# Another order of the opening's list, with 51 operations on other engines, in a chunked attention and two-layer expert kernel

## The chip, the core and the metric

The kernel runs on one core of a Trainium2 chip. A core has five engines that work side by side, each through its own instructions in the order in which they were written: PE (TensorE, matrix products and transposes), DVE (VectorE), ACT (ScalarE), POOL (GpSimd), and SP (SyncE), which here only issues DMAs. An instruction that must wait for another engine holds up everything behind it on its own engine. The metric is the time of one execution on the device in microseconds (us), median of several runs; less is better.

## The reference, cut to what matters

```python
# attention, per chunk of 32 queries: 8 memory keys, then 16 keys of left context, the chunk, 8 of right context
scores = scale * q_c @ k_full^T;  a = softmax(scores);  out[chunk] = a @ v_full      # (4, 8, 768, 64)
x = out as (3072, 512)
h = x @ w_in                                     # 512 -> 1024
solu = h * softmax(h);  ln = (solu - mean) / sqrt(var + 1e-6) * g_ln
x = ln @ w_out                                   # 1024 -> 512
h = x @ w2_in;  out = (h * clip(h + 3, 0, 6) / 6) @ w2_out    # 512 -> 2048 -> 512
```

The four weight matrices arrive as 64-bit floats, and the kernel turns them into 32-bit floats with integer operations. Products are made from a high part and a low part of each operand (three products for one).

## The kernel before, in words

The 3072 tokens are 24 tiles of 128. A tile passes through attention, the first layer and the second layer's first product; three tiles form a group for the product with `w_out`. The last stage, from about 423 us on, works through the 2048-wide layer and is not touched.

The work of the first seven tiles, the opening, stands in one list of names, `FIRST` (line 24 on). A loop near the end of the program calls one function for each entry, in the list's order; every function only appends instructions to its engines. So the list sets the order of the instructions on each engine and nothing else does: an engine never takes a later entry before an earlier one. From tile 7 (`STEADY`) a loop writes the instructions of each tile in a fixed pattern. A letter at an entry's end names its engine: A for ACT, D for DVE, P for POOL.

The entries that the text speaks of, with a tile number or a weight unit as the first argument:

- `load_q`, `load_k`, `load_v`, `load_mem_k`, `load_w1`, `load_wo`: DMAs, all issued by SP in the list's order. A `load_w1` is one of eight units of `w_in` (512 KB in two DMAs); unit u covers the columns u // 4 and the input rows u % 4. `load_k` is two DMAs (about 304 KB), `load_q` one of 256 KB, `load_v` eight to sixteen of 40 to 56 KB or less. There are two buffers for q, k and v, so `load_k:2` waits until `k_p:0` has read buffer 0.
- `w1_abs` (A or D), `w1_hold` (D or P), `w1_bits:u,0..2` (DVE): the conversion of one unit from 64 bits. `w1_hi` copies the rounded high part, `w1_lo` subtracts it (the low part). `wo_...` and `w2_...` do the same for the other weights, and `wo_g` multiplies by `g_ln`.
- `q_p`, `k_p`, `mem_p` (PE transposes of queries, keys, memory keys), with `q_e`, `k_e`, `mem_e`, `k_mem` as the copies out of the accumulator; `s_p` (PE, scores), `s_max`, `s_sub`, `s_sum` (DVE), `s_exp` (ACT), `s_norm` (D or P); `p_p` (PE transposes of the weights of attention, out of tile `pn`), `p_e` (copies), `v_p` (PE, attention output). `x_h` and `x_l` split that into high and low part.
- `m1:i,f,half` (PE): tile i times `w_in`, columns f, 12 matmuls or 6 for one half of the input rows. It needs `w1_hi` and `w1_lo` of its units and `x_h`, `x_l` of its tile. The first layer's nonlinearity and normalization follow as `ln_max` to `ln_norm`, `ln_p` (PE transposes), `ln_h`, `ln_l`; then `m2:g,piece` (PE, 8 matmuls with `w_out`).
- `warm:n` (PE, line 871): n transposes of the identity into a buffer that nobody reads. They compute nothing.
- `zero` clears buffers.

Of the kernel before, what the change touches and what calls it, by code (L numbers as in the profile page):

```python
# [22 lines left out]

STEADY = 7
FIRST = """
    load_q:0 load_w1:3 warm:10 q_p:0 warm:14 load_mem_k:0 mem_p:0 warm:6 mem_e:0,A zero:km0,D zero:v0,D zero:qb,P
    q_e:0,0,D w1_abs:3,D zero:kn0,P zero:kn1,D load_k:0 k_p:0,1 load_w1:7 load_mem_k:2 load_mem_k:3 load_w1:1 load_q:1
    w1_hold:3,P q_e:0,1,D k_p:0,0 warm:6 k_e:0,0,D k_mem:0,D mem_p:3 k_e:0,1,A s_p:0 warm:5 w1_abs:1,A w1_abs:7,A
    q_p:1 warm:8 q_e:1,1,A q_e:1,0,A zero:km1,D load_k:1 load_w1:0 load_k:2 load_w1:2 load_q:2 load_v:0 load_w1:6
    load_w1:5 load_w1:4 w1_bits:3,0 w1_bits:3,1 w1_hold:1,D mem_e:3,D w1_bits:3,2 s_edge:0 k_p:1,1 mem_p:2 k_p:1,0  # L30
    warm:6 s_max:0 w1_bits:1,0 s_sub:0 mem_e:2,A k_e:1,1,A k_e:1,0,A s_exp:0 s_p:1 warm:4 w1_abs:0,A w1_abs:2,A
    k_p:2,0 warm:6 k_e:2,0,A spread_mem_v:0,0,A zero:v1,P w1_hold:7,P w1_bits:7,0 w1_bits:1,1 w1_bits:7,1 w1_bits:1,2
    w1_bits:7,2 s_sum:0 w1_hold:0,D w1_bits:0,0 w1_bits:0,1 w1_hi:3,P s_norm:0,D zero:pb,P p_p:0 warm:6 q_p:2 load_k:3
    load_q:3 load_mem_k:1 load_q:4 load_v:1 p_e:0,0,A p_e:0,1,A spread_mem_v:0,64,A k_p:2,1 v_p:0 w1_bits:0,2
    w1_hi:1,D s_max:1 s_sub:1 s_exp:1 q_e:2,0,D x_h:0,0 k_e:2,1,D w1_hi:7,A w1_abs:6,A w1_abs:5,A w1_hold:2,P
    q_e:2,1,D s_p:2 warm:8 s_sum:1 w1_bits:2,0 w1_bits:2,1 s_norm:1,D p_p:1 warm:4 w1_bits:2,2 p_e:1,0,A w1_abs:4,A
    p_e:1,1,A w1_hi:2,A w1_lo:1,P w1_lo:3,P s_max:2 w1_hold:5,D x_l:0,0 w1_hold:4,D w1_bits:5,0 w1_bits:4,0
    w1_bits:5,1 load_k:4 load_wo:4 load_g load_v:2 consts w1_hi:0,P w1_lo:0,P w1_hold:6,P w1_lo:7,P w1_lo:2,P
    load_wo:2 m1:0,0,0 early_open k_p:3,1 k_p:3,0 k_e:3,1,A q_p:3 k_e:3,0,A q_e:3,1,A q_e:3,0,A w1_bits:4,1 s_sub:2
    w1_bits:6,0 w1_bits:5,2 mem_p:1 m1:0,0,1 s_p:3 q_p:4 w1_bits:6,1 w1_bits:4,2 w1_hi:4,D w1_bits:6,2 w1_lo:4,D  # L40
    w1_hi:5,P spread_mem_v:1,0,A s_exp:2 spread_mem_v:1,64,A v_p:1 w1_hi:6,D s_sum:2 s_max:3 s_norm:2,D s_sub:3
    q_e:4,1,A x_h:1,0 q_e:4,0,A mem_e:1,A w1_lo:5,P m1:0,1,0 w1_lo:6,P k_p:4,1 m1:0,1,1 x_l:1,0 k_e:4,1,D p_p:2
    k_p:4,0 m1:1,0,0 s_exp:3 ln_max:0 wo_abs:4,A wo_hold:4,D s_sum:3 wo_bits:4,0 s_norm:3,P load_wo:0 load_k:5
    load_wo:1 p_e:2,0,A k_e:4,0,A s_p:4 m1:1,0,1 ln_exp:0 p_e:2,1,A v_p:2 wo_abs:2,A wo_bits:4,1 ln_den:0 s_max:4
    ln_solu:0 wo_abs:0,D x_h:2,0 wo_hold:0,D wo_bits:4,2 s_sub:4 x_l:2,0 ln_mean:0 p_p:3 m1:1,1,0 k_p:5,0 m1:1,1,1
    m1:2,0,0 k_p:5,1 m1:2,0,1 s_exp:4 k_e:5,0,A ln_sq:0 p_e:3,0,A p_e:3,1,A wo_bits:0,0 s_sum:4 wo_g:4 wo_hold:2,P
    wo_bits:0,1 wo_hi:4,D ln_var:0 k_e:5,1,A wo_abs:1,A ln_max:1 wo_bits:0,2 ln_exp:1 wo_bits:2,0 ln_pow:0 wo_hold:1,D
    wo_bits:2,1 s_norm:4,P ln_norm:0 ln_den:1 load_q:5 load_v:3 load_k:6 m1:2,1,0 q_p:5 v_p:3 q_e:5,1,A q_e:5,0,A
    x_h:3,1 p_p:4 p_e:4,0,A load_wo:5 load_q:6 wo_abs:5,A p_e:4,1,A s_p:5 ln_p:0,0 ln_h:0,0,1 k_p:6,1 m1:2,1,1 k_p:6,0
    wo_bits:2,2 wo_g:0 ln_solu:1 ln_mean:1 wo_bits:1,0 wo_bits:1,1 wo_hi:0,D k_e:6,1,A q_p:6 k_mem:6,D ln_sq:1  # L50
    load_v:4 load_wo:7 v_p:4 load_q:7 load_wo:3 load_k:7 ln_max:2 wo_g:2 s_edge:5 q_e:6,1,A ln_exp:2 ln_var:1
    k_e:6,0,D wo_hi:2,D s_max:5 wo_lo:4,P x_l:3,1 wo_lo:0,P m1:3,0,0 x_h:4,1 ln_p:0,1 m1:3,0,1 m1:3,1,0 wo_hold:5,P
    q_e:6,0,A ln_den:2 wo_lo:2,D wo_bits:1,2 s_sub:5 s_p:6 q_p:7 k_p:7,0 m1:3,1,1 ln_l:0,0,1 x_l:4,1 ln_pow:1
    ln_solu:2 wo_bits:5,0 m1:4,0,0 wo_abs:7,A s_exp:5 ln_h:0,1,1 wo_hold:7,D wo_g:1 s_sum:5 s_norm:5,P s_edge:6
    wo_bits:5,1 ln_mean:2 k_e:7,0,A wo_abs:3,A wo_hold:3,P ln_l:0,1,1 ln_sq:2 wo_hi:1,A q_e:7,0,A q_e:7,1,A ln_norm:1
    ln_p:1,0 m1:4,0,1 k_p:7,1 p_p:5 m1:4,1,0 ln_max:3 ln_exp:3 ln_h:1,0,1 ln_p:1,1 m1:4,1,1 k_e:7,1,A wo_bits:5,2
    wo_lo:1,P load_v:5 load_wo:6 p_e:5,0,A wo_abs:6,D s_max:6 ln_den:3 ln_var:2 ln_pow:2 ln_l:1,0,1 s_sub:6 s_exp:6
    p_e:5,1,A ln_h:1,1,1 ln_l:1,1,1 ln_norm:2 wo_bits:3,0 ln_solu:3 load_k:8 k_p:8,1 ln_p:2,0 ln_h:2,0,1 ln_l:2,0,1
    s_p:7 k_e:8,1,A load_v:6 load_q:8 v_p:5 early_close k_p:8,0 ln_p:2,1 m2:0,0 wo_bits:3,1 wo_hold:6,D ln_max:4
    ln_exp:4 x_h:5,1 k_e:8,0,A s_sum:6 s_norm:6,P x_l:5,1 p_p:6 q_p:8 wo_bits:6,0 ln_den:4 ln_mean:3 ln_solu:4 m1:5,0  # L60
    s_max:7 wo_g:5 wo_bits:3,2 wo_g:3 wo_hi:5,P wo_lo:5,P wo_bits:6,1 wo_hi:3,D m1:5,1 s_sub:7 ln_mean:4 ln_h:2,1,1
    ln_l:2,1,1 q_e:8,1,A ln_sq:3 wo_lo:3,D wo_bits:6,2 m2:0,1 wo_bits:7,0 ln_var:3 wo_g:6 wo_bits:7,1 wo_bits:7,2
    wo_g:7 load_k:9 p_e:6,0,A p_e:6,1,A v_p:6 q_e:8,0,A ln_pow:3 ln_norm:3 wo_hi:6,A wo_lo:6,P s_exp:7 s_p:8 wo_hi:7,A
    wo_lo:7,P m2:0,2 m2:0,3 ln_p:3,0 m2:0,4 ln_p:3,1 x_h:6,1 ln_max:5 s_sum:7 x_l:6,1 s_norm:7,D p_p:7 m2:0,5 ln_sq:4
    ln_exp:5 ln_h:3,0,1 ln_h:3,1,0 ln_den:5 ln_solu:5 m1:6,0 ln_l:3,0,1 s_max:8 m2_e:0,0 m2:0,6 m2:0,7 m1:6,1 load_v:8
    load_w2:1 w2_abs:1,A w2_hold:1,P w2_bits:1,0 ln_mean:5 p_e:7,1,A ln_sq:5 p_e:7,0,D ln_var:5 ln_var:4 w2_bits:1,1
    ln_pow:4 ln_pow:5 w2_bits:1,2 ln_l:3,1,0 ln_norm:4 ln_p:4,1 load_v:7 v_p:7 ln_max:6 m2_e:0,1 s_sub:8 ln_norm:5
    ln_p:4,0 m2:0,8 m2:0,9 ln_exp:6 ln_h:4,1,0 x_h:7,0 ln_den:6 ln_l:4,1,0 ln_p:5,1 m2:0,10 ln_solu:6 x_l:7,0
    ln_mean:6 ln_p:5,0 m2:0,11 load_w2:3 w2_store:1 w2_abs:3,A s_exp:8 s_sum:8 ln_sq:6 ln_var:6 w2_hold:3,P ln_pow:6
    s_norm:8,P ln_norm:6 ln_h:5,1,0 load_w2:0 m2_s:0,1 w2_abs:0,A ln_h:4,0,0 w2_hold:0,P ln_l:4,0,0 ln_l:5,1,0  # L70
# [1016 lines left out]
```

## Time and profile before

| what | value |
|---|---|
| median of 3 runs (lowest, highest) | 924.26 us (923.72, 926.64) |
| the profiled execution | 925.95 us, its span 923.9 us |
| PE busy, share of the span | 903.0 us, 98% |
| DVE, ACT, POOL busy | 594.2, 450.5, 431.2 us |
| opening: start to the first matmul of tile 7 | 0 to 133.45 us |
| first matmul with `w_in` (tile `h`) | 33.92 us |

The span runs from the first to the last instruction that the profiler saw; 2.05 us of the execution lie outside it. "Busy" on PE includes the identity transposes. A row of the timeline gives start, length, engine, line, operation, tiles and, in square brackets, the time that the engine stood idle before it, with what ended that. PEclk is the clock granted to TensorE as a share of its full 2.4 GHz.

### The profile page before, as it was taken

Reading aid. Unit: us, or ns where it says so; the run is one execution under the profiler, and the core shown is the slowest. Engines: PE = TensorE matmul, PEld = TensorE weight load, DVE = VectorE, ACT = ScalarE, POOL = GpSimd, SP = SyncE. Lnnn points to the kernel's source line nnn. Section 1 sums busy time; section 2 is a strip of 40 time slices with the busy share of each in tenths; the row PEclk is TensorE's granted clock in tenths of the full one; section 3 lists DMA queues with packets and bytes.
Section 4 is the critical chain, followed back from the end, with each engine's and each line's share of the span. In section 5 each row is a group of like instructions: output and inputs, shape, how many; then the busy total and the mean of one; then the engine's idle time right before and its main releaser. Section 6 shows DMA issues by size and latency. Waiting matters only on the chain.

```text
span 923.9 us, 20340 instructions
## 1 busy us (share of the span) xinstructions
PE 903.0 (98%) x7823; PEld 848.0 (92%) x7823; DVE 594.2 (64%) x1043; ACT 450.5 (49%) x802; POOL 431.2 (47%) x465
## 2 busy tenths in 40 slices
...
GB/s 201 186 226 131 56 112 177 224 189 244 216 210 225 195 252 174 145 263 272 223 209 156 200 87 206 134 173 164 181 181 106 206 113 174 185 169 175 122 183 103
DMA packets 175627, 165.13 MB, mean 179 GB/s; under 512 B 107436, under 2 KB 128428, under 8 KB 175148
## 3 DMA queue, kind: packets, MB, share of 16 engines
...
q14 instruction: 33, 0.27, 0.1%
...
## 4 chain that ended last, share of the span: by engine, by line
PE 75%; DVE 10%; DMA 4%; issue 4%; POOL 3%; SPq 1%; ACT 1%; DVEq 0%; POOLq 0%; ACTq 0%
PE ph L771 25%; PE acc L825 23%; PE m L616 11%; PE h L531 9%; PE tp L588 2%; PE sc L444 2%; PE tp L500 1%; DMA b2d<-b_km 1%; PE tp L482 1%; DMA pair<-w2d 1%; PE tp L431 1%; SPq L193 1%; DMA w2raw<-in_moe_w_out_dram 1%; DVE so L557 1%; DVE so L581 1%
## 5 line engine op out<-in xcount | busy, mean ns | idle before, releaser
L531 PE MATMUL h<-w,xh 128*128 128x512 f32 x336 | 108.5, 403 | 1.0 <-DVE w L307 0.6
L616 PE MATMUL m<-lnh,wol 128*128 128x384 f32 x256 | 88.1, 344 | 1.0 <-POOL wol L344 0.7
L616 PE MATMUL m<-lnh,woh 128*128 128x384 f32 x256 | 87.9, 343 | 0.5 <-ACT woh L218 0.5
L616 PE MATMUL m<-lnl,woh 128*128 128x384 f32 x256 | 87.9, 343 | 0.0
L786 POOL TENSOR_TENSOR b_pe<-b_pe 128x128 f32<-128x128 f32 x48 | 27.0, 562 | 129.9 <-DVE b_pe L783 129.9
L786 POOL TENSOR_TENSOR b_pn<-b_pn 128x128 f32<-128x128 f32 x48 | 26.5, 552 | 124.0 <-DVE b_pn L783 123.1
L531 PEld LDWEIGHTS h<-w,xh 128*128 128x128 f32 x336 | 60.0, 188 | 12.7 <-DVE w L307 0.9
L246 DVE TENSOR_TENSOR b_ll<-b_xh,b_lh 128x512 fp32r<-128x512 f32 x48 | 33.2, 692 | 58.1 <-ACT b_lh L245 58.1
L576 POOL TENSOR_TENSOR lst<-lst,constants 128x1 f32<-128x1 f32 x24 | 15.2, 634 | 117.9 <-DVE lst L571 114.7
L771 PE MATMUL ph<-b_xah,b_wa 128*128 128x256 f32 x384 | 69.4, 276 | 0.0
L771 PE MATMUL ph<-b_x2r,b_wa 128*128 128x256 f32 x384 | 69.3, 276 | 0.0
L231 POOL TENSOR_SCALAR w2t<-w2t 128x512 f32<-128x512 f32 x32 | 62.1, 1947 | 14.3 <-ACT w2t L224 13.8
L246 DVE TENSOR_TENSOR b_wb<-b_xh,b_wb 128x512 fp32r<-128x512 f32 x48 | 38.5, 802 | 45.5 <-ACT b_wb L245 45.5
L531 PE MATMUL h<-w,xl 128*128 128x512 f32 x168 | 66.2, 394 | 1.3 <-DVE xl L261 1.3
L245 ACT ACTIVATE b_wb<-b_xh 128x512 fp32r<-128x512 f32 x48 | 30.3, 632 | 60.3 <-POOL b_xh L788 60.3
L771 PEld LDWEIGHTS ph<-b_xah,b_wa 128*128 128x128 f32 x384 | 59.6, 188 | 0.0
L771 PEld LDWEIGHTS ph<-b_x2r,b_wa 128*128 128x128 f32 x384 | 59.6, 188 | 0.0
L246 DVE TENSOR_TENSOR b_ll<-b_pe,b_lh 128x384 fp32r<-128x384 f32 x48 | 28.1, 586 | 47.6 <-ACT b_lh L245 47.5
L245 ACT ACTIVATE b_lh<-b_xh 128x512 fp32r<-128x512 f32 x48 | 30.3, 632 | 58.0 <-POOL b_xh L788 58.0
L246 DVE TENSOR_TENSOR b_xal<-b_pn,b_xah 128x384 fp32r<-128x384 f32 x48 | 26.8, 559 | 48.4 <-ACT b_xah L245 48.4
L245 ACT ACTIVATE b_xah<-b_pn 128x384 fp32r<-128x384 f32 x48 | 25.2, 525 | 60.8 <-POOL b_pn L786 59.5
L771 PE MATMUL ph<-b_xal,b_wa 128*128 128x256 f32 x192 | 53.0, 276 | 0.0
...
## 6 DMA issues: line engine op xcount, KB each, us to landing
...
```

The lines of the kernel that those rows point to most:

```text
L193: SP.dma_start(out=dst[r0 + NM + lo - s0:r0 + NM + hi - s0, j], in_=v[b, h0:h0 + 4, lo:hi, :].rearrange("h t d -> t h d"),)
L231: ENG[eng].tensor_scalar(out=tf, in0=tf, scalar1=U_LO, scalar2=U_HI, op0=ALU.max, op1=ALU.min)
L245: ACT.activation(out=hi, in_=r, func=AF.Copy)
L246: (eng or DVE).tensor_tensor(lo, r, hi.bitcast(F32), ALU.subtract)
L444: PE.matmul(sc[64 * x:64 * x + 64, c, s], qb[:, p, c].rearrange("k y t -> k (y t)"), kT[i % 2][:, p, c], start=True, stop=True)
L531: PE.matmul(h[:, f], a[:, kt], w[kt][:, f * 512:(f + 1) * 512], start=n == 0, stop=n == 3 * NKT - 1)
L576: POOL.tensor_tensor(st[:, 10:11], st[:, 9:10], mhalf, ALU.pow)
L588: PE.transpose(pt[:, c], so[:, fc * P:(fc + 1) * P], ident)
L616: PE.matmul(acc, w[fc // 2][:, fc % 2, dc * P:(dc + 1) * P], a[:, fc], start=n == 0, stop=n == len(todo) - 1)
L771: PE.matmul(ph[:, k], w[:, wl, dc * P:(dc + 1) * P], xg[gi][xl][dc], start=m == 0, stop=m == len(todo) - 1)
L786: POOL.tensor_tensor(q[:, 6], q[:, 0], q[:, 3], ALU.add)
L825: PE.matmul(out, a[al][:, blk], w[:, wl], start=j == 0 and m == 0 and PLACE[p][1] == 0, stop=j == NS - 1 and m == 2, skip_group_check=True)
```

## The change

`FIRST` is replaced as a whole; nothing else in the program differs. Both lists hold the same operations on the same data, except for the identity transposes: 83 in twelve entries before, 118 in ten entries now. 51 entries name another engine: from DVE to ACT 14, from DVE to POOL 15, from ACT to DVE 6, from POOL to DVE 7, from POOL to ACT 4, from ACT to POOL 5. DVE is thus rid of 29 and given 13, POOL is rid of 11 and given 20, ACT is rid of 11 and given 18. The order differs nearly everywhere; of the table the diff shows little:

```diff
-    load_q:0 load_w1:3 warm:10 q_p:0 warm:14 load_mem_k:0 mem_p:0 warm:6 mem_e:0,A zero:km0,D zero:v0,D zero:qb,P
+    zero:kn1,D zero:km1,D load_q:0 zero:v0,D zero:qb,P load_w1:0 load_mem_k:0 zero:kn0,P zero:km0,D load_k:0
...
+    warm:30 s_p:1 load_w1:7 w1_bits:6,1 w1_abs:4,A w1_hi:5,A load_k:2 w1_hi:0,A warm:3 q_p:2 s_norm:0,P s_max:1
+    w1_hold:4,D warm:27 k_p:2,0 load_q:3 w1_bits:4,0 w1_abs:7,A k_p:2,1 w1_bits:4,1 zero:pb,P s_sub:1 q_e:2,0,A
...
```

SP's list now begins with: `load_q:0`, `load_w1:0`, `load_mem_k:0`, `load_k:0`, `load_k:1`, `load_w1:5`, `load_q:1`, `load_w1:6`, `load_w1:4`, `load_q:2`, `load_w1:7`, `load_k:2`, `load_q:3`, `load_w1:2`, `load_k:3`, `load_v:0`, `load_w1:1`, `load_k:4`, `load_q:4`, `load_mem_k:3`, `load_w1:3`, `load_v:1`, `load_wo:1`, `load_k:5`. Before, the units of `w_in` came as 3, 7, 1, 0, 2, 6, 5, 4, and the second, third and fourth key tile behind more of them.

Place one is PE around the scores of the second tile (`s_p:1`). `idle` is the tile of the identity transposes, `sc` that of the scores, `q_raw`, `kn0` and `km` hold queries and keys as loaded. Before:

```order
L871 MATMUL idle_359<-ident_73 128x128 x6
L444 MATMUL sc_375<-kT_142,qb_140 64x64 x16
L871 MATMUL idle_392<-ident_73 128x128 x4
L402 MATMUL tp_399<-ident_73,kn0_135 128x128
L403 MATMUL tp_399<-ident_73,km_137 128x24
```

Now:

```order
L431 MATMUL tp_301<-ident_73,q_raw_246 128x128 x4
L871 MATMUL idle_318<-ident_73 128x128 x30
L444 MATMUL sc_349<-kT_142,qb_140 64x64 x16
L871 MATMUL idle_377<-ident_73 128x128 x3
L431 MATMUL tp_381<-ident_73,q_raw_316 128x128 x4
L871 MATMUL idle_391<-ident_73 128x128 x27
```

60 identity transposes stand where 10 stood, and `q_p:2` is drawn ahead of the third tile's keys.

Place two is PE ahead of the first matmul with `w_in` (tile `h`); `pn` is read by `p_p:1`, `v0` by `v_p:0`. Before:

```order
L500 MATMUL tp_473<-pb_141,v0_138 64x2x32 x16
L444 MATMUL sc_507<-kT_142,qb_140 64x64 x16
L871 MATMUL idle_524<-ident_73 128x128 x8
L482 MATMUL tp_540<-ident_73,pn_538 128x128 x4
L871 MATMUL idle_545<-ident_73 128x128 x4
L531 MATMUL h_592<-w1_240,xh_498 128x512 x2
```

Now the keys of the fifth tile (`k_p:4`, eight instructions, of which the first two stand here) lie between `p_p:1` and `h`:

```order
L871 MATMUL idle_545<-ident_73 128x128 x5
L500 MATMUL tp_551<-pb_141,v0_138 64x2x32 x16
L444 MATMUL sc_576<-kT_142,qb_140 64x64 x16
L482 MATMUL tp_593<-ident_73,pn_500 128x128 x4
L871 MATMUL idle_598<-ident_73 128x128 x2
L402 MATMUL tp_601<-ident_73,kn0_135 128x128
L403 MATMUL tp_601<-ident_73,km_137 128x24
```

`sc_507` holds the scores of the third tile, `sc_576` those of the fourth: one more tile has been transposed and scored before `h` begins.

Place three is DVE around `x_l:0` (line 261, tile `xl`), which the first `h` matmuls need. `w1raw` holds units of `w_in` in conversion: line 226 is `w1_abs`, 231 `w1_hold`, 235, 238 and 241 are `w1_bits`. Before:

```order
L456 TENSOR_REDUCE ast_557<-sc_507 128x8
L231 TENSOR_SCALAR w1raw_239<-w1raw_239 128x512
L261 TENSOR_TENSOR xl_499<-tp_473,xh_498 128x512
L231 TENSOR_SCALAR w1raw_312<-w1raw_312 128x512
L235 TENSOR_SCALAR w1raw_239<-w1raw_239 128x512
```

Now:

```order
L238 SCALAR_TENSOR_TENSOR w1raw_291<-w1raw_291 128x512
L226 TENSOR_SCALAR w1raw_242<-w1raw_242 128x512
L231 TENSOR_SCALAR w1raw_242<-w1raw_242 128x512
L261 TENSOR_TENSOR xl_607<-tp_551,xh_606 128x512
L235 TENSOR_SCALAR w1raw_242<-w1raw_242 128x512
L238 SCALAR_TENSOR_TENSOR w1raw_242<-w1raw_242 128x512
```

`xl` now stands behind the first two steps of unit 1 (`w1raw_242`), and so behind that unit's DMA.

## Rows read from the trace of the kernel before

**Rows 1.** The page, part 1: busy us (share of the span) and instructions of each engine

```profile
PE 903.0 (98%) x7823; PEld 848.0 (92%) x7823; DVE 594.2 (64%) x1043; ACT 450.5 (49%) x802; POOL 431.2 (47%) x465
```

**Rows 2.** Windows: stretch, its length, busy us of engines (instructions), PEclk, DMA share, GB/s

```profile
0.00:14.10 14.10, 11.99 (x96) 10.20 (x97) 5.90 (x11) 2.69 (x5) 4.86 (x10) 1.00 0.87 196
14.10:33.92 19.82, 14.90 (x174) 12.61 (x173) 18.43 (x34) 11.01 (x20) 12.76 (x12) 0.91 0.94 213
33.92:112.00 78.08, 73.48 (x681) 56.59 (x680) 76.75 (x136) 54.60 (x97) 44.39 (x33) 1.00 0.58 141
112.00:133.45 21.45, 21.45 (x152) 20.00 (x152) 14.64 (x34) 10.81 (x20) 7.79 (x8) 1.00 0.45 128
133.45:423.00 289.55, 288.47 (x2405) 257.07 (x2405) 230.40 (x422) 160.62 (x295) 115.74 (x95) 1.00 0.71 209
```

**Rows 3.** Waits of PE, 0 to 133.4 us: us in total, times, longest

```profile
PE tp L482 <- DVE pn L474: 4.1, 2, 3.0
...
PE h L531 <- DVE xl L261: 1.3, 1, 1.3
...
PE h L531 <- DVE w L307: 0.6, 1, 0.6
```

**Rows 4.** Timeline of PE, 0 to 134 us: start, length, line, operation, count, idle before

```profile
1.34 2.40 PE L871 MATMUL idle<-ident 128*128 128x128 f32 x10 [1.34 <-POOL ident masks.py:199]
...
17.54 0.87 PE L871 MATMUL idle<-ident 128*128 128x128 f32 x6
...
24.62 1.12 PE L482 MATMUL tp<-ident,pn 128*128 128x128 f32 x4 [3.04 <-DVE pn L474]
...
33.92 0.71 PE L531 MATMUL h<-w,xh 128*128 128x512 f32 x2
...
36.95 0.27 PE L402 MATMUL tp<-ident,kn 128*128 128x128 f32 x1
...
38.60 0.66 PE L431 MATMUL tp<-ident,q_raw 128*128 128x128 f32 x4
39.19 0.41 PE L389 MATMUL tp<-ident,mk 8*128 8x8 f32 x4
39.52 0.73 PE L531 MATMUL h<-w,xh 128*128 128x512 f32 x2
...
41.11 1.15 PE L444 MATMUL sc<-kT,qb 128*64 128x64 f32 x32
...
133.45 0.63 PE L531 MATMUL h<-w,xh 128*128 128x512 f32 x2
```

**Rows 5.** Groups by line and shape, DVE, 0 to 150 us: busy us, mean ns, idle before

```profile
L235 DVE TENSOR_SCALAR w1raw<-w1raw 128x512 uint32<-128x512 uint32 x8 | 5.8, 735 | 0.1
...
L474 DVE TENSOR_TENSOR pn<-pe,ast 128x512 f32<-128x512 f32 x4 | 3.2, 789 | 0.0
L220 DVE COPY qb<-tp 64x512 f32<-64x512 f32 x4 | 2.8, 688 | 3.6 <-PE tp L431 3.5
...
L220 DVE COPY kT<-tp 128x448 f32<-128x448 f32 x4 | 2.5, 620 | 1.4 <-PE tp L403 1.4
L220 DVE CAST woh<-woraw 128x512 fp32r<-128x512 f32 x3 | 2.4, 784 | 0.0
```

**Rows 6.** The same view for POOL

```profile
L231 POOL TENSOR_SCALAR w1raw<-w1raw 128x512 f32<-128x512 f32 x4 | 8.6, 2155 | 14.3 <-ACT w1raw L224 9.3 <-DVE w1raw L226 5.0
...
L474 POOL TENSOR_TENSOR pn<-pe,ast 128x512 f32<-128x512 f32 x5 | 5.6, 1114 | 10.9 <-DMA kn<-in_k_dram 6.0 <-DVE ast L470 4.9
```

**Rows 7.** Timeline of DVE, 11 to 18 us

```profile
11.46 0.35 DVE L235 TENSOR_SCALAR w1raw<-w1raw 128x512 uint32<-128x512 uint32 x1
...
17.06 1.70 DVE L235 TENSOR_SCALAR w1raw<-w1raw 128x512 uint32<-128x512 uint32 x1
```

**Rows 8.** Timeline of POOL beside it

```profile
16.98 0.60 POOL L220 CAST w<-w1raw 128x512 fp32r<-128x512 f32 x1
17.53 0.95 POOL L856 MEMSET pb<- 128x1024 f32 x1
```

More of the change, by code (lines that the diff above doesn't have):

```diff
@@ L25 @@
 FIRST = """
-    load_q:0 load_w1:3 warm:10 q_p:0 warm:14 load_mem_k:0 mem_p:0 warm:6 mem_e:0,A zero:km0,D zero:v0,D zero:qb,P
[L27 to L70, printed above, removed]
@@ L71 @@
-    ln_h:5,0,0 ln_l:5,0,0 load_q:9 m2_s:0,0 m2_e:0,2 m2_e:0,3 m2_s:0,2 m2_s:0,3 load_v:9 load_k:10
+    zero:kn1,D zero:km1,D load_q:0 zero:v0,D zero:qb,P load_w1:0 load_mem_k:0 zero:kn0,P zero:km0,D load_k:0
+    w1_abs:0,D load_k:1 warm:26 mem_p:0 q_p:0 mem_e:0,A q_e:0,0,D warm:2 k_p:0,0 k_e:0,0,D k_mem:0,D q_e:0,1,A
+    w1_hold:0,P k_p:0,1 k_e:0,1,A load_w1:5 load_q:1 warm:6 s_p:0 w1_bits:0,0 k_p:1,1 w1_bits:0,1 w1_bits:0,2
+    w1_abs:5,D s_edge:0 k_p:1,0 k_e:1,0,A w1_hold:5,P s_max:0 load_w1:6 k_e:1,1,D s_sub:0 w1_bits:5,0 w1_abs:6,A
@@ new lines @@
+    load_w1:4 q_p:1 w1_bits:5,1 s_exp:0 q_e:1,1,D w1_bits:5,2 s_sum:0 w1_hold:6,P w1_bits:6,0 q_e:1,0,A load_q:2
+    warm:30 s_p:1 load_w1:7 w1_bits:6,1 w1_abs:4,A w1_hi:5,A load_k:2 w1_hi:0,A warm:3 q_p:2 s_norm:0,P s_max:1
+    w1_hold:4,D warm:27 k_p:2,0 load_q:3 w1_bits:4,0 w1_abs:7,A k_p:2,1 w1_bits:4,1 zero:pb,P s_sub:1 q_e:2,0,A
+    s_exp:1 w1_bits:6,2 w1_bits:4,2 load_w1:2 q_e:2,1,A s_sum:1 k_e:2,0,A w1_hold:7,P load_k:3 p_p:0 q_p:3 k_e:2,1,A
+    p_e:0,0,A w1_bits:7,0 load_v:0 w1_hi:6,P s_p:2 w1_bits:7,1 w1_hi:4,A w1_bits:7,2 w1_abs:2,A q_e:3,0,A w1_hold:2,D
```

37 lines of the change are left out of this document (added).

## The prediction

> **What bounds the kernel now.** I first looked at the busy shares of the page: PE is busy in 98% of the span [rows 1]. So the kernel is shortened only where PE waits, or where it works for nothing. The windows show where that is [rows 2]. The lengths of the first four windows less their busy time give 11.6 us without PE work up to 133.45 us, where tile 7 and the fixed loop begin [rows 4]. In the 289.55 us behind that PE lacks only 1.1 us, so whatever the opening gains arrives at the end nearly whole. Of the 11.6 us, 7.0 lie before the first `h` matmul at 33.92 us and 4.6 behind it. The first 1.34 us, until the identity exists, cannot go [rows 4]; 5.7 us are left of the early part, and 10.3 us in all.
>
> Who ends these waits? The view of PE's waits names DVE for the largest: 4.1 us for `pn` (the two `p_p`, 3.04 us of it ahead of the first), 1.3 us for `xl`, 0.6 us for a low part of `w` [rows 3]. That fits the windows: DVE is busy 18.4 of 19.8 us before the first `h` and 76.8 of 78.1 us behind it [rows 2]. From 112 us on DVE has time (14.6 of 21.5 us) and PE has no gap. The opening is thus bound by DVE's queue and PE together.
>
> **The change part by part.**
>
> *Identity transposes.* Six take 0.87 us, 0.145 us each [rows 4]; 35 more cost 35 x 0.145 = 5.1 us of PE time in any case, since they are instructions in line and are not skipped when the data is there. All other PE work is the same. So the most that the opening can gain is 10.3 - 5.1 = 5.2 us, and every wait that the new order has (beyond the 1.34 us) is taken off that: gain = 5.2 - early waits - late waits.
>
> *PE ahead of the first `h`.* The order puts two more key tiles, one query tile and one set of scores there, and two `mem_p` less. By the starts of neighbouring rows a key tile takes 38.60 - 36.95 = 1.65 us, a query tile 0.59, a `mem_p` 0.33, and the scores about 1.1 [rows 4]: 3.3 + 0.6 + 1.1 - 0.7 = 4.3 us. That is work drawn forward, not added. Without any early wait the first `h` would start at 33.92 - 5.7 + 5.1 + 4.3 = 37.6 us, against 33.92 + 4.3 = 38.2 for the same amount of work done before. The early part is therefore nearly a wash: 5.7 us of waits are exchanged for 5.1 us of identity transposes.
>
> *The waits that go.* `s_norm:0` and `s_norm:1` leave DVE's full queue for POOL, and `p_p:0` stands behind 60 identity transposes (8.7 us) and two more transposing steps, so its 3.04 us wait is covered. `x_l:0` now waits on DVE for unit 1 of `w_in`, and its reader is due at 37.6 us. SP has issued about 6.4 MB up to that unit (7 units of 0.52 MB, four query and four key tiles, one value tile). At the rates of the first two windows, 196 GB/s to 14.1 us (2.76 MB) and 213 GB/s after it [rows 2], it lands at 14.1 + 3.63 / 0.213 = 31.1 us; three DVE instructions of some 0.4 to 0.8 us later [rows 5] `xl` is there, at about 33. That wait (1.3 us) and that for the low part (0.6 us) should go too. What queues behind DVE's wait for unit 1 is that unit's own conversion and `s_sum:2`; their readers on PE come after the first twelve `h` matmuls.
>
> *The new early waits.* Two places can wait. `mem_p:0` is reached at about 6.7 us, and its data was used at 7.4 us before, with the same DMAs ahead: 0 to 0.7, I take 0.5. `k_p:5` stands behind `load_v:1` and a whole unit of `w_out` in SP's queue, 8.8 MB in all. PE reaches it about 8.3 us after the first `h` (three times six matmuls of 1.6 us, 0.6 + 0.3 + 1.1 + 1.1 + 0.4 for the rest), at 45.9. At 213 GB/s throughout it lands at 42.5 us; with 213 to 33.92 us and the 141 GB/s of the third window behind that [rows 2] at 46.9. So 0 to 1.0 us, I take 0.5. Early waits: 1.0 us.
>
> *DVE's load and the late waits.* DVE is rid of 16 instructions net, of 0.62 to 0.79 us by their groups [rows 5]: 16 x 0.7 = 11 us. POOL gets 9 net, at 1.1 us (`s_norm`) to 2.2 us (`w1_hold`) each [rows 6]: 10 to 19 us on top of the 70 us that it is busy in the opening [rows 2], so it has room. What POOL's instructions do to DVE is the cost that the diff hides. A `w1_bits` step that is 0.4 us short as a rule took 1.70 us from 17.06 us on [rows 7], and ended just behind two POOL instructions that ran from 16.98 to 18.48 us [rows 8]. Its group has a mean of 0.735 us [rows 5], so on average an instruction of that kind loses a quarter of what this one lost. If each of the 9 cost DVE nothing, DVE keeps 11 us; if each cost 1.3 us, 9 x 1.3 = 11.7 us eat all of it. I take a quarter, 3 us, nearest to the group's mean: DVE is about 8 us lighter, while PE comes to the same work at most 3 us earlier. Of the 4.6 us of late waits, 1.9 have gone above; of the other 2.7 I keep half, 1.3 us.
>
> The Trainium skill speaks against this change here: its page "SBUF — State Buffer", section "Who interferes with whom", says that VectorE in its two-port modes and GpSimd share one pair of ports as an exclusive lock, and that whichever is second stands still until the first has finished. Rows 7 and 8 agree with it for one instruction (1.70 us). Taken for all 9 it would return the whole 11 us to DVE; with the group's mean it returns 3 us. The rival on POOL below is what it would do here.
>
> *The end of the opening.* `load_v:8` is now issued last, behind the store of the last `w_out` result. Its reader stands some 10 us of PE work into the loop; I take it as covered.
>
> *Sum.* 5.2 - 1.0 - 1.3 = 2.9 us. The profiled execution would go from 925.95 us (span 923.9 us) to 923.05 us. It lies 1.7 us over the median of the three runs shown, which all lie within 3 us, so I take the difference off the median: 924.26 - 2.9 = 921.4 us. A measurement of this kernel can tell about 0.3%, 2.8 us, from no change, so this is just at that line.
>
> **The rivals.**
>
> *POOL takes back what DVE gives.* The 9 added POOL instructions block DVE fully, as the one at 17.06 us was. DVE's load is then 0.6 us above before, the late waits stay near 4.3 us, and the gain is 5.2 - 1.0 - 4.3 = -0.1: 924.4 us. For it: DVE is 97% full in the stretch where most of these instructions lie [rows 2]. Against it: the group's mean, and POOL is idle in more than a third of that stretch, so the instructions can fall beside DVE work that is not touched. The same time comes out if the change only swaps the owners of waits.
>
> *The loads come too late; slower.* In front of `h` PE now has identity transposes in place of waits that would shorten by themselves when something else is late. `k_p:5` and the value tile ahead of it hang on 8.8 MB, in a queue in which `load_v:1` must also wait for a clearing by POOL, behind four `w1_hold`. It decides below 6.05 / (45.9 - 14.1) = 190 GB/s after 14.1 us; at 150 GB/s, near the third window's 141, the keys land at 54.4 us, PE waits 8.5 us, and the gain is 5.2 - 0.5 - 1.3 - 8.5 = -5.1: 929.4 us. It passes the 0.3% line at about 159 GB/s. For it: the rate did fall to 141 GB/s from 33.92 us on. Against it: SP then asked for less (DMA share 0.58), and with more asked it gave 213 GB/s at 0.94.
>
> **How the numbers follow.** The forecast with its waits of 0.2 to 4.6 us, 919.1 to 923.7 us, gets 0.61, of which 0.45 lie below 921.5 (faster by over 0.3%) and 0.16 above. POOL's rival gets 0.25 (0.22 same, 0.01 faster, 0.02 slower), the late loads 0.14 (0.12 slower, 0.02 same). Faster 0.46, same 0.40, slower 0.14. The range runs from 918.6, just past the gain of 5.2 us, to 928.0, which leaves out the larger part of the late loads, about 1 in 10.
>
> **What would show it right or wrong.** In the profile of the changed kernel the first `h` matmul should start between 37.6 and 39.5 us and the first matmul of tile 7 at about 130.5 us. No wait of over 1 us should stand ahead of a `p_p` or for `xl`. DVE should be busy about 8 us less up to there. Waits of PE on the loads of keys or values of tiles 1 to 5 of several us mean the second rival. DVE's `w1_bits` and `wo_bits` with means above 0.9 us, and waits of PE on DVE, mean the first. The sum is wrong at its root if PE's gaps behind 133 us grow by what the opening saved.

## The result and the profile after

| | before | after |
|---|---|---|
| median of 6 runs (lowest, highest) | 924.62 us (923.72, 926.64) | 931.01 us (927.9, 931.8) |
| the profiled execution, its span | 925.95, 923.9 us | 931.8, 930.0 us |
| first matmul with `w_in` (`h`) | 33.92 us | 39.83 us |
| first matmul of tile 7, end of the opening | 133.45 us | 137.41 us |
| first matmul of the last stage (`ph`) | 423.79 us | 428.11 us |

The changed kernel is slower by 0.6%: ratio 1.006, 95% interval 1.0045 to 1.0075. Of the 6.1 us by which the span grew, 4.0 arise in the opening, and only 0.4 between it and the last stage. The other 1.7 us arise in the last stage, which the change does not touch; they are treated at the end.

Windows of the kernel after, with the columns and four of the five stretches of [rows 2] (stretch, length, busy us of PE, PEld, DVE, ACT, POOL with instructions, PEclk, DMA share, GB/s):

```profile
0.00:14.10 14.10, 11.39 (x96) 9.61 (x97) 8.02 (x16) 3.12 (x5) 5.56 (x10) 1.00 0.90 212
14.10:33.92 19.82, 17.42 (x207) 15.09 (x205) 19.30 (x27) 12.63 (x23) 15.37 (x13) 1.00 0.91 201
33.92:112.00 78.08, 72.33 (x648) 57.30 (x650) 66.08 (x116) 52.08 (x93) 49.31 (x40) 0.93 0.57 141
112.00:133.45 21.45, 20.81 (x164) 19.07 (x159) 15.99 (x31) 11.65 (x20) 10.04 (x9) 1.00 0.26 70
```

Length less PE's busy time gives 2.7 + 2.4 + 5.8 + 0.6 = 11.5 us without PE work, where it was 11.6 [rows 2]. So no wait was saved: they changed their owners and their places. By this count the opening is longer because PE is *busy* longer, 125.9 us up to 137.41 where it was 121.8 up to 133.45: 35 more identity transposes, and a granted clock of 0.93 in the third stretch (1.00 in [rows 2]; the 0.91 of the second stretch there is now 1.00). That says where the time stands and not yet what caused it; `e7_fewer` below shows that identity transposes can fill time that PE would otherwise have waited. DVE is busy 10.7 us less in the third stretch, where it now waits itself, and 0.9 us more in the second, where it was already full.

Waits of PE in the kernel after, 0 to 137.4 us (in total, times, longest), to be read against [rows 3]:

```profile
PE tp L402 <- DMA kn<-in_k_dram: 4.0, 1, 4.0
PE sc L444 <- DVE pe L461: 3.1, 2, 2.8
PE tp L389 <- DMA mk<-in_mem_k_dram: 1.4, 1, 1.4
...
PE m L616 <- POOL wol L344: 0.6, 1, 0.6
```

The waits for `pn`, `xl` and the low part of `w` are gone, as forecast. Two others stand in their place. The timeline of PE (start, length, line, operation, count, idle before) shows them, and what PE does behind them:

```profile
13.98 3.44 PE L871 MATMUL idle<-ident 128*128 128x128 f32 x30
17.35 1.15 PE L444 MATMUL sc<-kT,qb 128*64 128x64 f32 x32
...
34.86 1.88 PE L444 MATMUL sc<-kT,qb 128*64 128x64 f32 x32 [2.82 <-DVE pe L461]
...
51.88 0.30 PE L402 MATMUL tp<-ident,kn 128*128 128x128 f32 x1 [4.05 <-DMA kn<-in_k_dram]
...
53.01 1.22 PE L531 MATMUL h<-w,xh 128*128 128x512 f32 x2
...
58.43 1.36 PE L500 MATMUL tp<-pb,v 128*64 128x64 f32 x32
```

The same scores take 1.15 us at 17.35 and 1.88 behind the 2.82 us wait; the first two `h` matmuls behind the 4.05 us wait take 1.22 us instead of 0.73 [rows 4]. Both waits are followed by some microseconds at the lower of the two clock levels (1.2 instead of 2.4 GHz): the granted clock is 0.54 from 34.86 to 36.70 us and 0.50 from 53.01 to 58.43 us.

*Where the 4.05 us come from.* They stand ahead of `k_p:5`. SP's timeline in the kernel after (L320 is `load_wo`, L171 `load_k`), SP's own waits, and two windows with the columns as above:

```profile
37.28 2.54 SPq L193 DMA_DIRECT2D v<-in_v_dram  x4
46.56 0.36 SPq L320 DMA_DIRECT2D woraw<-in_moe_w_out_dram  x1
47.01 0.39 SPq L171 DMA_DIRECT2D kn<-in_k_dram  x1
```

```profile
SPq L320 <- POOL w L307: 3.7, 1, 3.7
SPq L320 <- DVE w1raw L241: 2.9, 1, 2.9
```

```profile
42.00:45.00 3.00, 3.00 (x16) 2.33 (x15) 1.79 (x4) 2.94 (x6) 2.97 (x4) 1.00 0.00 0
...
48.00:51.88 3.88, 0.00 (x0) 0.03 (x1) 2.67 (x6) 2.02 (x4) 0.00 (x0) 1.00 0.89 213
```

SP stood for 6.6 us at `load_wo:1`. What it had issued before went on until about 41 us; then the DMA engines moved nothing, 0 GB/s from 42 to 46.5 us, while PE still had work. PE's own wait follows at 47.83 us, when the keys are under way at 213 GB/s. The raw tile of `load_wo:0` and `load_wo:1` takes the buffer `lh1` (`BIG[2]` at line 312), which is also the raw tile of `w_in`'s units 2 and 6 (`BIG[kt]` at line 279). So `load_wo:1` waits for the last reader of unit 2, `w1_lo:2` (L307 on POOL). The keys of `k_p:5` come next in the list: issued at 47.01 us, read by PE from 51.88 on.

*Where the 2.82 us come from.* There is one accumulator for scores. `s_p:3` needs it back from `s_sub:2` (L461 on DVE), behind a row of DVE steps that took longer than such steps do [rows 5] while POOL worked. Timeline of DVE in the kernel after, then of POOL:

```profile
30.95 2.38 DVE L235 TENSOR_SCALAR w1raw<-w1raw 128x512 uint32<-128x512 uint32 x1
33.25 0.67 DVE L456 TENSOR_REDUCE ast<-sc 128x8 f32<-128x512 f32 x1
34.03 0.69 DVE L461 TENSOR_TENSOR pe<-sc,ast 128x512 f32<-128x512 f32 x1
```

```profile
30.45 1.72 POOL L307 TENSOR_TENSOR w<-w1raw,w 128x512 fp32r<-128x512 f32 x1
32.10 0.95 POOL L856 MEMSET v<- 128x1024 f32 x1
```

The step of L235, 0.735 us in the mean before, took 2.38 us and ended 0.3 us behind POOL's two; `s_max:2` and `s_sub:2` stood behind it.

### The profile page after: what moved, and what is told of

Same layout as the page of the kernel before. It is cut to its first block, busy times and chain, and to the rows that moved or that the text cites. A ratio compares the mean times of both kernels' runs of the same rounds, so it can differ in the third digit from the quotient of the medians.

```text
span 930.0 us, 20418 instructions
## 1 busy us (share of the span) xinstructions
PE 908.3 (98%) x7858; PEld 854.9 (92%) x7858; DVE 591.8 (64%) x1027; ACT 454.0 (49%) x809; POOL 441.7 (47%) x474
## 4 chain that ended last, share of the span: by engine, by line
PE 78%; DVE 9%; DMA 4%; issue 3%; POOL 2%; SPq 2%; ACT 1%; DVEq 0%; POOLq 0%; ACTq 0%
PE ph L771 27%; PE acc L825 24%; PE m L616 10%; PE h L531 9%; PE tp L500 2%; PE tp L588 2%; PE sc L444 2%; SPq L193 1%; DMA pair<-w2d 1%; PE tp L482 1%; DMA b_t<-w2d 1%; DMA woraw<-in_moe_w_out_dram 1%; DVE so L557 1%; PE tp L431 1%; DVE woraw L238 1%
## 5 line engine op out<-in xcount | busy, mean ns | idle before, releaser
L231 POOL TENSOR_SCALAR w2t<-w2t 128x512 f32<-128x512 f32 x30 | 57.7, 1933 | 2.7 <-ACT w2t L224 2.6
L788 POOL TENSOR_TENSOR b_xh<-b_pn 128x256 f32<-128x256 f32 x48 | 53.9, 1123 | 0.0
```

The lines of the kernel that those rows point to most:

```text
L231: ENG[eng].tensor_scalar(out=tf, in0=tf, scalar1=U_LO, scalar2=U_HI, op0=ALU.max, op1=ALU.min)
L788: POOL.tensor_tensor(s[:, 2:4], q[:, 1:3], q[:, 0:4:3], ALU.subtract)
```

## The experiments

Each was timed in five rounds beside the kernel before, whose medians were 925.03, 924.57 and 925.06 us in the three groups (`e1` to `e4`, `e5` to `e8`, `e9` to `e12`). "First `h`" and "`ph`" are read from the profiled execution.

| kernel | median (lowest, highest), us | ratio to before, 95% | first `h` | `ph` |
|---|---|---|---|---|
| the change | 931.01 (927.9, 931.8) | 1.006 (1.0045, 1.0075) | 39.83 | 428.11 |
| e1_loads | 924.94 (923.03, 928.78) | 0.9993 (0.9978, 1.0008) | 36.54 | 421.25 |
| e2_scores | 928.39 (927.14, 931.65) | 1.0033 (1.0019, 1.0046) | 36.41 | 426.82 |
| e3_both | 924.47 (921.89, 928.05) | 0.9997 (0.9981, 1.0013) | 36.47 | 419.87 |
| e4_fill | 929.65 (927.96, 932.6) | 1.0046 (1.0031, 1.0061) | 37.90 | 426.20 |
| e5_engines | 940.66 (940.17, 942.32) | 1.0171 (1.015, 1.0192) | 42.04 | 438.51 |
| e6_order | 936.61 (934.68, 937.5) | 1.012 (1.01, 1.0139) | 40.72 | 435.17 |
| e7_fewer | 923.79 (920.62, 926.86) | 0.9976 (0.9956, 0.9996) | 36.76 | 418.23 |
| e8_xl | 923.4 (922.02, 924.59) | 0.9981 (0.9967, 0.9996) | 36.17 | 420.21 |
| e9_lock | 922.57 (919.4, 925.61) | 0.997 (0.9953, 0.9986) | 37.50 | 421.64 |
| e10_xl_lock | 923.12 (920.12, 926.16) | 0.9974 (0.996, 0.9989) | 35.83 | 422.36 |
| e11_mem | 923.79 (920.9, 925.67) | 0.9979 (0.9967, 0.999) | 34.60 | 423.59 |
| e12_all | 923.78 (919.16, 928.16) | 0.9983 (0.9966, 1.0001) | 36.83 | 424.50 |

The "first `h`" must be read with care. The change, `e1` and `e4` have the same instructions in the same order on every engine ahead of it, and it starts at 39.83, 36.54 and 37.90 us; `e8` and `e11` are alike up to there too, and it starts at 36.17 and 34.60. The difference is there from early on: the wait for the first memory keys is 1.36, 0.27 and 0.95 us in the first three. With one profile of each kernel, differences of this size in that column cannot be put down to an edit.

**One DMA later on SP's list.**

```diff
-    p_e:1,1,A load_wo:1 k_e:4,1,A load_k:5 w1_hi:1,A s_sum:2 load_mem_k:1 s_norm:2,P load_g ...
-    s_max:3 load_v:2 mem_p:3 ...
+    p_e:1,1,A k_e:4,1,A load_k:5 w1_hi:1,A s_sum:2 load_mem_k:1 s_norm:2,P load_g ... s_max:3
+    load_v:2 load_wo:1 mem_p:3 ...
```

> The changed kernel with one entry moved: load_wo:1 stands behind load_v:2, so the DMAs of the sixth key tile (k_p:5), of memory keys, g_ln and of the third value tile are issued ahead of it. Theory 'SP stands at load_wo:1 until its buffer is given up by w1_lo:2': the wait of 4.05 us ahead of k_p:5 at 51.9 us falls under 1 us, the clock stays near 1.00 there, and the span falls by 5 to 7 us, to about 925 us. Rival 'the transfers themselves are too slow' (the one on record): the keys still land at 51 us or later, the wait stays over 3 us, and the time stays within 1.5 us of 931. Rival 'DVE bounds this stretch': the wait goes, another of the same size on DVE takes its place before 65 us, and the time stays at 929 to 931.

By the medians the whole loss is gone: 924.94 us against 931.01. In this kernel SP issued the keys at 38.77 us, and PE read them at 44.48 without a wait (timeline of SP, then of PE):

```profile
38.77 0.39 SPq L171 DMA_DIRECT2D kn<-in_k_dram  x1
...
44.48 0.27 PE L402 MATMUL tp<-ident,kn 128*128 128x128 f32 x1
```

So the rate of the transfers was not the limit, and no wait of that size on DVE took the place; the largest behind the first `h` is 1.23 us, for memory keys at 51.18 us. `ph` starts 6.9 us earlier than in the change, but only 3.6 us of that lie behind the first `h` (384.7 us from there to `ph`, where it was 388.3). The other 3.3 us lie ahead of it, where the two programs are the same. So the trace accounts for 3.6 of the 6.1 us between the medians; where the rest comes from stays open. What the slow clock behind the wait costs is asked for with `e4_fill`.

**The scores earlier on DVE.**

```diff
-    ... s_norm:1,P p_e:0,1,A load_w1:1 w1_lo:4,D ... w1_lo:6,P spread_mem_v:0,64,A s_max:2 ... s_sub:2 warm:5 ...
+    ... s_norm:1,P s_max:2 s_sub:2 p_e:0,1,A load_w1:1 w1_lo:4,D ... w1_lo:6,P spread_mem_v:0,64,A ... warm:5 ...
```

> The changed kernel with two entries moved: s_max:2 and s_sub:2 stand right behind s_norm:1 in the list, ahead of the steps for the weights of units 1, 4 and 2 that stood before them on DVE. Theory 'the scores of the fourth tile wait for the one accumulator of scores, which DVE gives up late': the wait of 2.82 us at 34.9 us falls under 1 us, and the clock stays at its upper level from 34 to 46 us; 2.8 us and some 1.4 us of slow clock go, but k_p:5 is then reached 4 us earlier and waits longer for a DMA that hangs on w1_lo:2, so that the end gains 0 to 1.5 us: 929.5 to 931. Rival 'the two waits are independent': the end gains 3 to 4 us, 927 to 928.

928.39 us, 2.6 below the change: between the two, nearer to the rival. The wait for the scores is gone (2.00 and 2.93 us of it are left in `e1` and `e4`, which do not make this move), but 3.4 us of waiting for the keys of `k_p:5` remain, and behind a 1.1 us wait for earlier keys, which had been hidden, the granted clock is 0.62 from 36 to 40 us. That `h` starts 3.4 us earlier proves nothing: in `e1`, without this move, it is 3.3.

**Both moves.**

> The changed kernel with both moves (load_wo:1 behind load_v:2; s_max:2 and s_sub:2 behind s_norm:1). Theory that the two waits and the slow clock behind each are the whole of the loss: 4.05 + 2.82 us of waits and about 4.5 us of slow clock go, 11 us at most; some 2 us come back as waits on DVE, and the time is 920 to 923 us. Rival 'DVE and POOL hold the opening, the two waits only show where': new waits on DVE take the place, and the time is 926 to 930 us.

924.47 us: neither. Two moves are no better than the first alone, within the intervals: the gains over the change, 6.1 and 2.6 us alone, are 6.5 together. Ahead of `h` the timeline of PE shows what comes next, `x_l:0` on DVE, and a slow clock behind it once more (1.22 us for the first `h` pair):

```profile
35.35 0.33 PE L402 MATMUL tp<-ident,kn 128*128 128x128 f32 x1 [1.52 <-DVE xl L261]
...
36.47 1.22 PE L531 MATMUL h<-w,xh 128*128 128x512 f32 x2
```

**The wait filled, SP's queue left alone.**

```diff
-    ... s_max:4 load_mem_k:2 k_p:5,1 load_wo:3 ...
+    ... s_max:4 load_mem_k:2 warm:36 k_p:5,1 load_wo:3 ...
```

> The changed kernel with 36 more identity transposes right ahead of k_p:5, in the place of its 4.05 us wait (36 x 0.11 us = 4.0 us, by the long rows of the changed kernel). Nothing else is moved, so SP's queue and the keys' landing stay. Theory 'half of the loss is the lower clock granted after the wait': the clock stays near 1.00 from 48 to 60 us, k_p:5 to v_p:5 take the shorter times that they had before, and the time falls by 2 to 3 us, to about 928.5. Rival 'the clock does not follow the wait, or costs nothing that is not hidden': within 0.7 us of the changed kernel.

The times leave it open: 1.4 us below the change, with intervals that overlap. The trace shows that the clock stayed up, and that the gain did not last. Timeline of PE in this kernel:

```profile
34.46 1.15 PE L444 MATMUL sc<-kT,qb 128*64 128x64 f32 x32 [2.93 <-DVE pe L461]
...
45.75 4.09 PE L871 MATMUL idle<-ident 128*128 128x128 f32 x36
...
51.31 0.73 PE L531 MATMUL h<-w,xh 128*128 128x512 f32 x2
...
54.24 1.15 PE L500 MATMUL tp<-pb,v 128*64 128x64 f32 x32
56.40 0.41 PE L389 MATMUL tp<-ident,mk 8*128 8x8 f32 x4 [1.00 <-DMA mk<-in_mem_k_dram]
...
62.66 0.63 PE L431 MATMUL tp<-ident,q_raw 128*128 128x128 f32 x4 [1.06 <-DMA q_raw<-in_q_dram]
```

From the first `h` behind the keys to `v_p` it is 54.24 - 51.31 = 2.93 us here and 58.43 - 53.01 = 5.42 in the change, for the same matmuls. The granted clock in these stretches is 1.00 here and 0.50 in the change. So the slow clock behind the wait made that work 2.5 us longer, and with filler in the place of the wait it did not, though SP stood as before. But PE then waits 1.00 us for memory keys and 1.06 us for queries, of which the change has only 0.45 for the queries, and from the first `h` to `ph` the two kernels take the same 388.3 us. The 1.9 us by which `ph` starts earlier all lie ahead of the first `h`. That the clock is worth 2.5 us at the end is thus not shown.

**Letters alone, order alone.** `e5` puts the 51 engine letters of the change into the order of before, `e6` the letters of before into the order of the change; for instance, in `e5`:

```diff
-    s_norm:0,D ... s_norm:1,D
+    s_norm:0,P ... s_norm:1,P
```

> The order of before with the 51 engine letters of the changed kernel (83 identity transposes, SP's queue as before). Theory 'the loss comes from the order, that is from where load_wo:1 and the scores of tile 2 stand': no wait of PE on keys over 0.5 us, and a time within 1.5 us of before, 923.5 to 926.5. Rival 'the letters cost it: POOL's added instructions lock DVE': waits of PE on pn, pe or xl grow ahead of the first h, DVE's w1_bits take over 0.9 us in the mean there, and the time is 928 to 931.

> The order of the changed kernel (118 identity transposes, its SP queue) with the engine letters of before. Theory 'order': the wait ahead of k_p:5 stays at 3 us or more, since load_wo:1 still waits for w1_lo:2 on POOL, and the time is 929 to 932. Rival 'letters': with s_norm:0 and s_norm:1 back on DVE and the copies back in place, PE's waits go under those of before, and the time is 924 to 926.

Both are far worse than either whole kernel, 940.66 and 936.61 us: in time, theory and rival missed in both. In `e5` the wait of the rival, for `pn`, is there, but also one of 2.5 us on keys. `e6` keeps the wait on keys (5.0 us), as the theory of the order says, but has 2 us waits on DVE besides. Waits of PE in `e5`, 0 to 60 us:

```profile
PE sc L444 <- ACT qb L218: 2.9, 1, 2.9
PE tp L403 <- DMA km<-in_k_dram: 2.5, 1, 2.5
PE h L531 <- POOL w L307: 2.5, 2, 2.3
PE tp L482 <- POOL pn L474: 2.1, 1, 2.1
```

ACT, the DMAs and POOL all show up as owners. Letters and order seem to be fitted to each other (argued from these two, not tested further), and half of the change tells little of the whole. It does not follow from these two which half "costs" the 6 us; `e1` answers that.

**Identity transposes.** `e3_both` without its two long rows.

```diff
-    warm:30 s_p:1 ...
-    w1_hold:4,D warm:27 k_p:2,0 ...
+    s_p:1 ...
+    w1_hold:4,D k_p:2,0 ...
```

> The version with both moves (load_wo:1 behind load_v:2; s_max:2 and s_sub:2 behind s_norm:1), without the two long rows of identity transposes, 30 and 27 (6.3 us of PE time at 0.11 us each). Theory 'ahead of the first h DVE sets the pace, and the identity transposes only fill PE's waits': the first h starts within 0.7 us of 36.5, PE's waits ahead of it grow by 5 to 6 us, part of the stretch runs at the lower clock, and the time stays within 1.5 us of that version, 923 to 926. Rival 'identity transposes are PE time in any case', as in the prediction on record: the first h starts about 6 us earlier and the time falls to 918 to 920.

First `h` at 36.76 against 36.47 us with 57 more of them: the 6.3 us of work are not on the path, and the time is not measurably another. Where they stood PE now waits, and what it does takes longer at the lower clock, 0.66 in this window where `e3_both` has 1.00 (timeline and window of `e7_fewer`):

```profile
16.74 1.97 PE L444 MATMUL sc<-kT,qb 128*64 128x64 f32 x32 [2.92 <-ACT qb L218]
```

```profile
14.10:33.92 19.82, 15.98 (x169) 13.03 (x171) 19.16 (x29) 13.75 (x24) 15.17 (x13) 0.66 0.94 207
```

**`x_l:0` earlier on DVE**, on top of `e3_both`.

```diff
-    ... w1_bits:2,1 ... w1_abs:1,D k_e:3,1,A w1_hold:1,D ... zero:v1,P x_l:0,0 ...
+    ... k_e:3,1,A ... zero:v1,P x_l:0,0 w1_bits:2,1 w1_abs:1,D w1_hold:1,D ...
```

> The version with both moves, and x_l:0 ahead of w1_bits:2,1, w1_abs:1 and w1_hold:1 in DVE's queue (by its trace these three took 2.4 us right ahead of x_l:0). Theory 'the wait of 1.5 us for xl at 35.4 us and the lower clock behind it, until 42 us, are what is left of the loss': first h at about 34.5 to 35, clock 1.00 from 34 to 60 us, and the time falls by 3 to 4 us, to 920.5 to 921.5. Rival 'the conversion of unit 1 and 2 on DVE is late then': PE waits for a low part of w before 50 us for as long as was gained, and the time stays at 923.5 to 925.5.

923.4 us, a third of the gain that was expected, and the interval overlaps with that of `e3_both`. The 1.5 us wait for `xl` went, but the clock did not stay up, as the theory had it: from 36.17 to 40.00 us it is 0.55, though no wait ahead of it is longer than 0.5 us. Waits on DMAs appeared, the second of them for memory keys whose DMA stands behind `load_wo:1` (timeline of PE):

```profile
34.46 0.33 PE L402 MATMUL tp<-ident,kn 128*128 128x128 f32 x1 [0.47 <-DMA kn<-in_k_dram]
...
36.17 0.95 PE L531 MATMUL h<-w,xh 128*128 128x512 f32 x2
...
51.93 0.38 PE L389 MATMUL tp<-ident,mk 8*128 8x8 f32 x4 [1.54 <-DMA mk<-in_mem_k_dram]
```

**POOL's steps back on DVE**, on top of `e3_both` (`e9`) and of `e8_xl` (`e10`).

```diff
-    s_norm:0,P   w1_lo:0,P   s_norm:1,P   w1_lo:6,P   w1_lo:5,P   w1_lo:7,P
+    s_norm:0,D   w1_lo:0,D   s_norm:1,D   w1_lo:6,D   w1_lo:5,D   w1_lo:7,D
```

> The version with both moves (load_wo:1 behind load_v:2; s_max:2 and s_sub:2 behind s_norm:1), with the six two-input POOL steps between 17.8 and 33.4 us given to DVE: s_norm:0, s_norm:1, w1_lo:0, 6, 5, 7. On DVE they would cost 6 x 0.68 = 4.1 us more. Theory 'a two-input step on POOL stops DVE for its length, so it relieves DVE of nothing': DVE's rows in that stretch go back to 0.4 to 0.7 us (there, six rows took 1.26 to 1.65 or 0.94 us, some 4.8 us too long in all), x_l:0 starts within 1 us of 34.6, and the time stays within 1.5 us of that version, 923 to 926. Rival 'POOL's share is a relief, as far as it was counted in the prediction (three quarters of it)': x_l:0 starts 3 us later and the time is 927 to 928.

> The version with x_l:0 drawn ahead on DVE, with the same six POOL steps given to DVE. Theory of the stop: DVE as fast as without, first h within 1 us of 36.2, time within 1 us of that version's 923.4. Rival: first h 3 us later, 926 to 927.

`e9` has the lowest median, 922.57 us, clear of the change and of before, but not of `e3_both` or of its other neighbours, whose intervals overlap with its own. Five of the six steps stand ahead of `x_l:0` on DVE (`w1_lo:7` comes behind it), 5 x 0.68 = 3.4 us of added work, and `x_l:0` starts at 35.72 us against 34.61, 1.1 us later. In `e10` it starts at 32.52 us against 33.17 in `e8`, but DVE was 0.8 us ahead there from the start of the stretch: the five steps cost about 0.1 us. The timelines of `e3_both` (DVE, then POOL) show why:

```profile
22.15 1.28 DVE L241 SCALAR_TENSOR_TENSOR w1raw<-w1raw 128x512 uint32<-128x512 uint32 x2
...
24.06 1.26 DVE L469 TENSOR_SCALAR ast<-ast 128x8 f32<-128x8 f32 x1
...
25.89 1.43 DVE L238 SCALAR_TENSOR_TENSOR w1raw<-w1raw 128x512 uint32<-128x512 uint32 x1
27.36 1.65 DVE L241 SCALAR_TENSOR_TENSOR w1raw<-w1raw 128x512 uint32<-128x512 uint32 x1
```

```profile
21.57 1.92 POOL L231 TENSOR_SCALAR w1raw<-w1raw 128x512 f32<-128x512 f32 x1 [1.84 <-ACT w1raw L224]
...
24.02 1.28 POOL L307 TENSOR_TENSOR w<-w1raw,w 128x512 fp32r<-128x512 f32 x1
25.73 1.04 POOL L474 TENSOR_TENSOR pn<-pe,ast 128x512 f32<-128x512 f32 x1 [0.44 <-DVE ast L470]
26.74 1.72 POOL L307 TENSOR_TENSOR w<-w1raw,w 128x512 fp32r<-128x512 f32 x1
```

The same three DVE steps in `e9_lock`:

```profile
25.75 0.17 DVE L469 TENSOR_SCALAR ast<-ast 128x8 f32<-128x8 f32 x1
...
26.48 0.69 DVE L238 SCALAR_TENSOR_TENSOR w1raw<-w1raw 128x512 uint32<-128x512 uint32 x1
27.21 0.69 DVE L241 SCALAR_TENSOR_TENSOR w1raw<-w1raw 128x512 uint32<-128x512 uint32 x1
```

Each long DVE step ends at most 0.55 us behind the POOL step beside it (25.32 and 25.30, 27.32 and 26.77, 29.01 and 28.46 us): it looks as if it had stood for most of the time that POOL worked. A 0.17 us step on 8 columns became 1.26 us. The Trainium skill's page "SBUF — State Buffer", section "Who interferes with whom", says that VectorE in its two-port modes and GpSimd share a pair of ports, which the first to come holds for its whole instruction while the other is blocked. These three rows agree, though no run here shows in which mode the steps ran. Not every POOL step does this: beside the clamp of `w1_hold` (L231, 21.57 to 23.49 us) the two L241 steps took 0.64 us each, no longer than the 0.69 of `e9_lock`.

**What is next behind the keys.** `e11_mem` issues the memory keys ahead of `load_wo:1` too; `e12_all` is that without the two long rows of identity transposes.

```diff
-    load_v:2 load_wo:1 mem_p:3 ... load_mem_k:2 k_p:5,1 ...
+    load_v:2 load_mem_k:2 load_wo:1 mem_p:3 ... k_p:5,1 ...
```

> The version with x_l:0 drawn ahead, and load_mem_k:2 issued behind load_v:2, ahead of load_wo:1 (its reader mem_p:2 waited 1.54 us at 51.9 us). Theory 'the wait is the place in SP's queue, as with k_p:5': it goes, nothing takes its place, and the time falls by 1 to 1.5 us to about 922. Rival 'PE would wait there for DVE anyway': no change, 923.4 within 0.7.

> The last one without the two long rows of identity transposes (30 and 27). Theory 'they only fill PE's waits ahead of the first h': within 1 us of the version with them. Rival 'identity transposes are PE time in any case': 5 to 6 us faster. Should the lower clock that they keep away reach behind the first h: 1 to 3 us slower.

923.79 and 923.78 us: nothing gained, and again nothing lost or won by 57 identity transposes. In `e11` the 1.54 us wait went and one of 3.28 us took its place at the next query tile (timeline of PE); in `e12`, where the same wait is 2.77 us, the trace names the DMA of the queries as its cause.

```profile
57.15 0.84 PE L431 MATMUL tp<-ident,q_raw 128*128 128x128 f32 x4 [3.28 <-DVE wot L238]
```

So the rival had the time, but not the reason that it gave, DVE: that DMA stands in SP's list behind eight of values and is issued only at 53.35 us in `e11` and 55.64 in `e12`. There the next entries of the same queue set the wait.

## Why the prediction was wrong

*The step that failed is the new early wait for `k_p:5`*, put at 0.5 us between 0 and 1.0. It was worked out from bytes and rate alone, 8.8 MB at 141 or 213 GB/s. What SP's instructions ahead of it must wait for was asked for `load_v:1` and not for `load_wo:1`, whose buffer is that of a unit of `w_in` still in conversion. The wait was 4.05 us, because SP stood for 6.6 us ahead of the keys and issued them only at 47.01 us; and `e1`, which moves that one entry, takes the whole loss away by the medians (3.6 us of it seen in the trace). It does not bring the 2.9 us of gain that were forecast: `e1` is level with before, 0.9993 (0.9978 to 1.0008), and has waits that the sum had no terms for, 2.00 us for the accumulator of scores and 1.23 us for memory keys.

*No term for the clock.* A wait was priced at its length. Behind the 4.05 us wait the work up to `v_p` took 2.5 us longer at the lower clock (`e4` against the change), and the scores behind the 2.82 us wait took 1.88 instead of 1.15 us. What of this reaches the end is open, since `e4` gave its gain back.

*Identity transposes, 5.1 us, were mis-sized.* In long rows one takes 0.11 us (3.44 us for 30), not 0.145; and, more important, `e7` shows that 57 of them are not on the path to the first `h`, where PE waits instead if they are left out. Ahead of it DVE is busy 19.2 of 19.8 us in `e7`. The bound "gain = 5.2 less waits" treated PE as the limit in a stretch where it was waiting for DVE.

*PE ahead of the first `h`.* 37.6 us was forecast and 39.83 came; that these lie near each other is luck. Less the first 1.34 us the forecast is 36.3 us of work without a wait. PE was busy 33.8 us up to there, part of it at the lower clock, and 32.7 us in `e1`, at a clock of 1.00; so the work was put some 3.6 us too high. About 1 us of that is the identity transposes, and rows of before in a stretch with a clock of 0.91 were taken as they stood. Against it stand waits of 4.7 us, of which 0.5 were forecast; the largest, 2.82 us for the accumulator of scores, had no term.

*The waits that go* (`pn`, `xl`, low part) went, as predicted. *`mem_p:0`*: 0.5 predicted, with a bound of 0.7; 1.36 us measured in the change, and 0.27 to 0.97 in the profiles of the variants that show it as a wait.

*DVE's load.* Up to the first matmul of tile 7 DVE is busy 112.7 us, where it was 115.7: 3 us lighter, against 8 predicted. The relief lies behind 33.92 us, where DVE now waits itself; in the 20 us ahead of that, where it was already full, it is busier by 0.9 us. There the price of a POOL step was not a quarter of a full stop: with five of them back on DVE, 3.4 us of work, `x_l:0` came only 1.1 us later (`e9` against `e3`), or 0.1 (`e10` against `e8`). The first rival was thus right on the mechanism, in that stretch; its price for the whole kernel, 924.4 us, was not the loss.

*Late waits.* Apart from the wait for the keys, PE waits 1.4 us behind the first `h` in the opening; 1.3 were predicted. `load_v:8` is covered, as predicted: between the opening and the last stage only 0.4 us were lost.

*The rival on late loads* had the place, the sign and, at 929.4 us, nearly the size, but the last by luck. Its mechanism was another: a rate below 190 GB/s. The rate was 213 GB/s once SP had issued the keys, and 0 from 42 to 46.5 us, while it stood.
